# Attention scores from two halves of PE's rows instead of stacked operands, with transfers, a square and norm steps at other times

## The chip, the cores and the metric

One core of a Trainium2 chip runs the whole program. The metric is the device time of one execution in microseconds (us). The kernel before was run three times: 1136.16, 1132.1 and 1135.2 us, so its median is 1135.2 us. One more execution was profiled; it took 1132.5 us.

## The reference, cut to what matters

```python
q_rot, k_rot = (rotate(q), rotate(k))            # q, k, v: (4, 8, 576, 64) float32
scores = scale * np.matmul(q_rot, k_rot.transpose(0, 1, 3, 2))
scores = scores - np.max(scores, axis=-1, keepdims=True)
attn = np.exp(scores)
attn = attn / (np.sum(attn, axis=-1, keepdims=True) + 1e-09)
x = np.matmul(attn, v)                           # then to 2304 tokens x 512
xn = x / rms * rms_g
x = (silu(xn @ w_gate) * (xn @ w_val)) @ w_out   # d_ff 1536
x = (((x @ w1) * (x @ w2)) @ w3) @ w_out2        # d_ff 1024
```

q, k, v and the result are float32; most weights arrive as float64 and are converted on the chip. For the accuracy of float32 on PE, the kernel splits an operand into a rounded part ("hi") and the rest ("lo") and adds the products hi*hi, hi*lo and lo*hi (the tuple `PASS`).

## The kernel before, in words

**Stages.** The attention runs first, over 16 pairs of heads (two heads of 64 columns lie one under the other on the 128 partitions). Then the gated layer runs over 6 blocks of 384 tokens (lines 789 to 997; block 0 in two halves with block 1 between them), each with 12 columns n of 128 features: `pair_mm` is 24 matmuls, `second` 12. The products with w1, w2, w3 and w_out2 follow.

**One pair of heads.** POOL rotates q and k two pairs ahead (steps ra to rd). PE turns the result (q0p, q1p, q2p), ACT writes the hi part to `xs` and DVE the lo part to `ys` (the h and l steps), both in one tile `xy`. q occupies columns 0 to 703 of it, k the last 576. Then transfers of SP's queue build the operands of the scores. `q1d` (line 437) makes the stack of q, `qst`: for a head, hi on 64 rows and lo on the other 64. `q2d` (line 447) makes the stack of k, `ks`: hi on both halves of the rows, and lo on both halves. Each of the two steps issues four transfers. Pair 0 takes part of this by six copies of ACT and DVE instead (lines 728 to 734).

**Scores.** A pair has nine tiles of 128 queries: t = 0 to 3 of head 0, t = 5 to 8 of head 1, and t = 4 with what is left of both heads. The step S (line 471) makes a tile's 576 scores in two column halves `hf` of 288, each in its own PSUM bank. With the stacks, two matmuls over all 128 rows per half give the four products hi*hi, lo*hi, hi*lo and lo*lo: four matmuls a tile, eight for t = 4, 640 in all. M is the row maximum (DVE, line 487), E the exponential with its sum (ACT, line 493), T, H and Lo turn and split the tile (PE, ACT, DVE, lines 499 to 507), PV multiplies with v (line 555), X scales the result (POOL, line 612) and XD stores it.

**Order.** In the attention the order of every engine and of SP's queue is written out by hand. `ORDER` gives each step of a pair a time in units of one tile (nine to a pair); steps in q and v run one pair ahead, ra to rd, lq and lv two. `ONCE` does it for single steps: WF.u fetches the weight unit u, NX loads the rows of the first norm block, sq2 squares one of them. Of the steps that issue transfers, lq stands at 0.641, q1d at 5.817, q2d at 6.798, lv at 16.571 and XD at 17.967 (in the next pair's count 7.57 and 8.97); NX stands at 48.023 (pair 5, 3.02) and WF.5 at 94.711 (pair 10, 4.71), the other WF outside 0.5 to 7.2 of their pairs. The entry fixes only who stands before whom on an engine or in the queue. An instruction whose inputs are late holds up whatever stands behind it on the same engine or queue.

After the attention a scheduler orders the work by the order of the program, and gives a tile its buffer when one of its pool is free. The norm of block i+1 (`norm_steps`: load, three squares `sq`, `rst` and `nwt` for 1/rms, three scalings `zz`, line 668, and then xp, xh, xl three times) is cut by `NORM_AT` over the columns n of block i, for i = 2 to 4. The jobs of `JOBS` convert later weights (wo, w3, ws) and form sums of x (`sums`, lines 900 to 928) beside the blocks. The rows that a norm step loads, the outputs of a block and the tiles that the sums store to xsD share three buffers (pool `x2`, tag `o`). Each fetched weight goes through one of three raw buffers (`wst`) and each conversion through three `wt` buffers.

Of the kernel before, what the change touches and what calls it, by code (L numbers as in the profile page):

```python
# [9 lines left out]
F32R = mybir.dt.float32r  # L10
# [30 lines left out]
WARM = (22, 2, 3, 17)  # L41
NORM_AT = {5: (0, 1), 6: (1, 4), 7: (4, 6), 8: (6, 9), 9: (9, 12), 10: (12, 15), 11: (15, 18)}

# [17 lines left out]
def f(ap):  # L61
    return ap.bitcast(F32)
# [3 lines left out]
def kernel(  # L66
# [21 lines left out]
    nc = tc.nc  # L88
    B, H, S, D = q.shape
# [8 lines left out]
    HS = S // 2  # L98
# [57 lines left out]
    xy_p = pool("xy", 1)  # L156
    st_p = pool("st", 2)
# [117 lines left out]
    st = [0, 0]  # L275
# [20 lines left out]
    PASS = ((0, 0), (0, 1), (1, 0))  # L296
# [50 lines left out]
    part = {}  # L347
# [50 lines left out]
    QW = 704  # L398
    xy = xy_p.tile([128, 2, QW + S], F32R, name="xy")
    xs, ys = xy[:, 0], xy[:, 1]  # L400
    qst = [st_p.tile([128, 2, QW], F32R, name=f"qs{i}", bufs=1) for i in range(2)]
    qps = {}

    def two(a):
        return a[:, 576:832].rearrange("p (a b) -> p a b", a=2)[:, :, 0:64]

    def qt(g):

        n = [1, 4, 4][g]
# [8 lines left out]

        def qh(p):
            nc.scalar.copy(out=xs[:, c] if g else two(xs), in_=qps[p, g])  # L420

        def ql(p):
            hi, lo = (xs[:, c], ys[:, c]) if g else (two(xs), two(ys))
            nc.vector.tensor_tensor(out=lo, in0=qps.pop((p, g)), in1=f(hi), op=ALU.subtract)
# [6 lines left out]

    def move(mv):
        for o, i in mv:
            nc.sync.dma_start(out=f(o), in_=f(i))

    @step
    def q1d(p):
        qs = qst[p % 2]
        sl = slice(0, 640)
        sa = sl  # L440
        if p == 0:
            sa = slice(512, 640)
        move([(qs[0:64, 0, sa], xs[0:64, sa]), (qs[64:128, 0, sa], ys[0:64, sa]),
              (qs[64:128, 1, sl], xs[64:128, sl]), (qs[0:64, 1, sl], ys[64:128, sl])])

    @step
    def q2d(p):
        new_ks(p)
        ks = stacks[p]
        sl = slice(QW, QW + S)  # L450
        move([(ks[a:a + 64, 2 * h:2 * h + 2], xy[64 * h:64 * h + 64, :, sl]) for h in range(1 if p == 0 else 0, 2) for a in (0, 64)])

    def new_ks(p):
        if p not in stacks:
            stacks[p] = st_p.tile([128, 4, S], F32R, tag="ks", name="ks")

    s_ps, s_max, p_sb, sums, t_ps, l_ps, pv_ps, osb, xt, o_ps, rs_t = [{} for _ in range(11)]

    def hr(t):
        return (0, t) if t < 4 else (1, t - 5)  # L460
# [9 lines left out]
    def tile_steps(t):  # L470
        def S_(p):
            qs, ks = qst[p % 2], stacks[p]
            ps = ps_s.tile([128, 2, 512], F32, tag="s", name="s")
            if t == 4:
                mm = [(qs[:, h, 512 + 64 * h:640 + 64 * h], ks[:, 2 * h + i]) for h in range(2) for i in range(2)]
            else:
                h, r = hr(t)
                mm = [(qs[:, h, r * 128:(r + 1) * 128], ks[:, 2 * h + i]) for i in range(2)]
            n = len(mm)
            for hf in range(2):  # L480
                for i, (l, r_) in enumerate(mm):
                    nc.tensor.matmul(ps[:, hf, 0:HS], lhsT=l, rhs=r_[:, hf * HS:(hf + 1) * HS], start=(i == 0), stop=(i == n - 1))  # L482
            s_ps[p, t] = ps
# [216 lines left out]
    load_v(0)  # L700
    nc.vector.memset(f(xy[:, :, 512:576]), 0.0)
    for qs in qst:
        nc.vector.memset(f(qs[:, :, 640:QW]), 0.0)
    junk = const.tile([128, 1], F32, name="junk")
# [13 lines left out]
    for n_ in ("ra", "rb", "rc", "rd"):  # L718
        part[n_](1)
    new_ks(0)  # L720
    ks, sl = stacks[0], slice(QW, QW + S)
    for i, n_ in enumerate(("q2p", "q0p", "q1p")):
        part[n_](0)
        if i < 2:
            warm(i + 1)
    for n_ in ("q2h", "q0h", "q2l", "q0l", "q2d"):
        part[n_](0)
    nc.scalar.copy(out=ks[0:64, 0], in_=xs[0:64, sl])
    nc.vector.tensor_copy(out=ks[0:64, 1], in_=ys[0:64, sl])
    part["q1h"](0), part["q1l"](0)  # L730
    nc.scalar.copy(out=qst[0][0:64, 0, 0:512], in_=xs[0:64, 0:512])
    nc.vector.tensor_copy(out=ks[64:128, 1], in_=ys[0:64, sl])
    nc.scalar.copy(out=ks[64:128, 0], in_=xs[0:64, sl])
    nc.vector.tensor_copy(out=qst[0][64:128, 0, 0:512], in_=ys[0:64, 0:512])
    for n_ in ("q1d", "vh", "vl"):
        part[n_](0)
# [519 lines left out]
```

## Time and profile before

| | value |
|---|---|
| median of 3 runs | 1135.2 us (1132.1 to 1136.16) |
| profiled execution | 1132.5 us, span of its instructions 1130.7 us |
| mean granted clock of PE | 0.991 |
| PE matmul busy | 1085.4 us (96%), 6627 matmuls |
| DVE busy | 693.6 us (61%) |
| ACT busy | 558.3 us (49%) |
| POOL busy | 218.6 us (19%) |
| DMA | 183.52 MB, mean 162 GB/s |

An engine's share is a mean over stages with different limits: POOL works almost only in the attention, and DVE is near full there and half idle later. So the rows below are taken by stretch. Matmuls overlap one another, and the page says that a busy PE is not PE at its peak; the distance from one group of matmuls to the next in the chain of waits is the better measure of what one costs.

### The profile page before, as it was taken

The numbers are of one execution on the slowest core, as the hardware profiler recorded it, in microseconds if no ns is written. First come the engines' busy times: TensorE is split into PE (matmuls) and PEld (weight loads), VectorE is DVE, ScalarE is ACT, GpSimd is POOL, SyncE is SP. The second block draws the span as 40 slices with busy tenths as digits, with TensorE's granted clock in tenths as the row PEclk, the third lists the DMA queues.
The fourth block names the chain that finished last, engine by engine and source line by source line (L and its number), as shares of the span: only waits on it lengthen the run. The fifth ranks groups of instructions, "written<-read, shape, count | busy, mean of one in ns | idle before, by whom it ended". The sixth has DMA issues, their size and how long they took to land.

```text
span 1130.7 us, 18269 instructions
## 1 busy us (share of the span) xinstructions
PE 1085.4 (96%) x6627; PEld 1044.5 (92%) x6627; DVE 693.6 (61%) x1278; ACT 558.3 (49%) x1241; POOL 218.6 (19%) x191
## 2 busy tenths in 40 slices
PE   7899899799998999999899999999999999999998
PEld 6899899799997999999899999999999999987886
DVE  6999999799879883256666456653353442433221
ACT  4798898698875552234342243323454433323221
POOL 5777677579510000000000000000000000000000
PEclk9999999999999999999899999999999999999999
DMA  7677776767435640149476177554752324703451
GB/s 198 158 189 187 188 174 173 180 163 182 117 124 171 192 159 1 36 171 331 152 252 197 55 259 253 195 183 158 292 198 83 121 84 151 259 15 109 157 168 56
DMA packets 124698, 183.52 MB, mean 162 GB/s; under 512 B 18624, under 2 KB 85696, under 8 KB 124608
## 3 DMA queue, kind: packets, MB, share of 16 engines
q1 hardware_dynamic: 124608, 182.35, 53.2%
q8 instruction: 53, 0.87, 0.3%
q14 instruction: 37, 0.30, 0.1%
HBM read 101.63 MB, written 52.17 MB: 136 GB/s over the span
## 4 chain that ended last, share of the span: by engine, by line
PE 65%; DMA 14%; DVE 11%; issue 3%; ACT 2%; SPq 2%; POOL 2%; POOLq 0%; DVEq 0%; ACTq 0%
PE mm L305 16%; PE ps L1049 14%; PE ps L1190 9%; PE acc L813 8%; PE s L482 5%; PE ps L1152 4%; PE pv L555 3%; PE tp L499 3%; DMA wsD<-wt 3%; DMA wraw<-in_moe_w_val_dram 2%; DMA ks<-xy 2%; DVE nm L487 2%; DVE wt L233 1%; DMA woD<-wt 1%; DVE pt L507 1%
## 5 line engine op out<-in xcount | busy, mean ns | idle before, releaser
L305 PE MATMUL mm<-xc,wgv 128*128 128x384 f32 x1728 | 319.7, 337 | 3.2 <-ACT wgv L242 2.0
L305 PEld LDWEIGHTS mm<-xc,wgv 128*128 128x128 f32 x1728 | 302.3, 189 | 5.0 <-ACT wgv L242 3.2
L1049 PE MATMUL ps<-xs,cw 128*128 128x384 f32 x1008 | 175.9, 334 | 0.3 <-DMA xs<-xsD 0.3
L1049 PEld LDWEIGHTS ps<-xs,cw 128*128 128x128 f32 x1008 | 174.6, 188 | 1.0 <-DMA xs<-xsD 0.7
L813 PE MATMUL acc<-us,wo 128*128 128x384 f32 x864 | 166.8, 336 | 4.0 <-ACT us L104 3.6
L813 PEld LDWEIGHTS acc<-us,wo 128*128 128x128 f32 x864 | 150.4, 188 | 6.7 <-ACT us L104 5.6
L482 PE MATMUL s<-ks,qs 128*128 128x288 f32 x640 | 125.1, 324 | 17.0 <-DMA ks<-xy 7.6
L487 DVE TENSOR_REDUCE nm<-s 128x1 f32<-128x576 f32 x144 | 108.0, 750 | 17.8 <-PE s L482 16.1
L493 ACT ACTIVATE p<-s,nm 128x576 f32<-128x576 f32 x144 | 107.5, 746 | 21.2 <-DVE nm L487 20.5
L482 PEld LDWEIGHTS s<-ks,qs 128*128 128x128 f32 x640 | 94.3, 198 | 20.6 <-issue 12.5
L1190 PE MATMUL ps<-wp,us 128*128 128x512 f32 x432 | 98.2, 389 | 1.4 <-ACT us L104 1.4
L1190 PEld LDWEIGHTS ps<-wp,us 128*128 128x128 f32 x432 | 81.0, 188 | 18.6 <-ACT us L104 1.8
L507 DVE TENSOR_TENSOR pt<-tp,pt 128x512 fp32r<-128x512 f32 x144 | 94.7, 682 | 1.8 <-ACT pt L503 1.3
L104 ACT CAST us<-u 128x384 fp32r<-128x384 f32 x72 | 36.9, 512 | 112.5 <-DVE u L317 107.1
L317 DVE SCALAR_TENSOR_TENSOR u<-mm,sg 128x384 f32<-128x384 f32 x72 | 39.9, 555 | 82.5 <-PE mm L305 77.3
L555 PE MATMUL pv<-pt,vs 128*128 128x288 f32 x512 | 81.5, 301 | 2.4 <-DVE pt L507 2.4
L503 ACT CAST pt<-tp 128x512 fp32r<-128x512 f32 x144 | 82.5, 585 | 2.7 <-PE tp L499 1.7
L499 PE MATMUL tp<-idn,p 128*128 128x128 f32 x576 | 83.1, 277 | 0.6 <-DVE lt L537 0.5
L555 PEld LDWEIGHTS pv<-pt,vs 128*128 128x128 f32 x512 | 71.3, 189 | 2.9 <-DVE pt L507 2.9
L499 PEld LDWEIGHTS tp<-idn,p 128*128 128x128 f32 x576 | 68.9, 143 | 1.9 <-PE s L482 0.7
L315 ACT ACTIVATE sg<-mm 128x384 f32<-128x384 f32 x72 | 35.2, 489 | 65.5 <-PE mm L305 64.5
L1039 DVE TENSOR_TENSOR gv<-ps,gv 128x384 f32<-128x384 f32 x48 | 26.7, 556 | 54.9 <-PE ps L1049 34.2
(138 smaller groups left out, 1358.0 us busy)
## 6 DMA issues: line engine op xcount, KB each, us to landing
ks<-xy SPq DMA_DIRECT2D x62, 288.0 KB, 5.0
wraw<-in_moe_w_dram SPq DMA_DIRECT2D x32, 512.0 KB, 5.0
xsD<-xo SPq DMA_DIRECT2D x28, 384.0 KB, 3.8
xs<-xsD SPq DMA_DIRECT2D x14, 768.0 KB, 7.7
wraw<-in_moe_w_out_dram SPq DMA_DIRECT2D x20, 512.0 KB, 4.4
qs<-xy SPq DMA_DIRECT2D x62, 160.0 KB, 2.9
uD<-gv SPq DMA_DIRECT2D x12, 768.0 KB, 3.6
gv<-uD SPq DMA_DIRECT2D x24, 384.0 KB, 4.3
```

Of the source, the lines that this page charges most:

```text
L305: nc.tensor.matmul(ps[:, 0:CH], lhsT=w[:, a, s, c * 128:(c + 1) * 128], rhs=x[:, b_, c, :], start=(i == 0), stop=(i == 3 * KC - 1))
L482: nc.tensor.matmul(ps[:, hf, 0:HS], lhsT=l, rhs=r_[:, hf * HS:(hf + 1) * HS], start=(i == 0), stop=(i == n - 1))
L487: nc.vector.tensor_reduce(out=nm, in_=s_ps[p, t][:, :, 0:HS], axis=AX.XY, op=ALU.max, negate=True)
L493: nc.scalar.activation(out=pp.rearrange("p (a b) -> p a b", a=2), in_=s_ps.pop((p, t))[:, :, 0:HS], func=AF.Exp, bias=s_max.pop((p, t)), s ...
L499: nc.tensor.transpose(ps[:, c, :], p_sb[p, t][:, LF + c * 128:LF + (c + 1) * 128], idn)
L503: lastins["act"] = nc.scalar.copy(out=hi, in_=src)
L507: lastins["dve"] = nc.vector.tensor_tensor(out=lo, in0=src, in1=f(hi), op=ALU.subtract)
L555: nc.tensor.matmul(ps[:, 0:HS], lhsT=l.rearrange("p s d -> p (s d)"), rhs=r, start=(i == 0), stop=(i == 8))
L813: nc.tensor.matmul(acc[o][:, 0:CH], lhsT=wo[kind, n][:, a, o * 128:(o + 1) * 128], rhs=us[:, b_], start=(n == first and s == 0), stop=(n = ...
L1049: nc.tensor.matmul(b[ch], lhsT=w[i][:, p_, c * 128:(c + 1) * 128], rhs=x[i][:, r, c], start=(first and ch != 1 and n == 0), stop=(n == 5), ...
L1152: nc.tensor.matmul(p_, lhsT=t[a][:, c], rhs=woc[c][:, b_], start=(i == 0), stop=(i == 3 * NJ - 1))
L1190: nc.tensor.matmul(ac[o], lhsT=us[j // 2][:, a, j % 2, o * 128:(o + 1) * 128], rhs=wp[j][:, b_], start=(j == 0 and s == 0), stop=(j == NJ ...
```

## The change

The scores are computed from q and k where they were written. `xyt` holds two tiles in place of one `xy`, taken in turn by pairs. The stacks `qst` and `ks` are gone. `q1d` and `q2d` now issue two transfers each, which copy the tile with its two halves of rows exchanged into `stacks[p]`. A tile of scores takes the three products of `PASS`, each over 64 rows. For all pairs but the first, and for t = 4 of the first, column half 0 reads rows 0 to 63 and column half 1 rows 64 to 127: one of the two from the tile itself, the other from the exchanged copy. For t = 0 to 3 and 5 to 8 of pair 0 both column halves read the rows of their own head in the tile. That makes six matmuls a tile, twelve for t = 4, 960 in all, and lo*lo is no longer formed. The six copies of pair 0 are gone. `q1d` moves from 5.817 to 1.30 in `ORDER` and `q2d` from 6.798 to 1.45; `sq2` moves from 50.172 to 56.9 in `ONCE`. In `NORM_AT` the load of the rows moves from n = 5 to 3, the squares from 6 to 4, rst and nwt from 7 to 5, the scalings from 8 to 7.

```diff
@@ -22,7 +22,7 @@
     "E4": 2.051, "M5": 2.134, "Lo1": 2.149, "LH3": 2.471, "LL3": 2.5, "E5": 2.509, "H2": 2.685, "S6": 2.756,
     "M6": 2.821, "Lo2": 2.903, "T3": 3.161, "H3": 3.449, "S7": 3.7, "Lo3": 3.739, "E6": 4.29, "LP4": 4.29,
     "LH4": 4.474, "T4": 4.668, "S8": 4.729, "M7": 4.91, "H4": 5.08, "LL4": 5.462, "ra": 5.617, "E7": 5.756,
-    "q1d": 5.817, "M8": 6.032, "PV00": 6.229, "Lo4": 6.264, "rb": 6.41, "E8": 6.669, "q2d": 6.798, "OS00": 6.875,
+    "q1d": 1.30, "M8": 6.032, "PV00": 6.229, "Lo4": 6.264, "rb": 6.41, "E8": 6.669, "q2d": 1.45, "OS00": 6.875,
     "rc": 7.081, "LP8": 7.652, "rd": 7.781, "LH8": 8.249, "T5": 8.365, "T7": 8.385, "T8": 8.415, "H5": 8.594,
     "LL8": 8.681, "Lo5": 8.773, "T6": 8.824, "PV01": 8.959, "H7": 9.058, "H8": 9.103, "Lo7": 9.166, "H6": 9.477,
     "Lo8": 9.545, "OS01": 9.588, "vh": 9.685, "Lo6": 9.742, "PV11": 10.964, "vl": 11.081, "RS": 11.858, "OS11": 11.89,
@@ -32,14 +32,14 @@
 ONCE = {"WF.0": 0.058, "WF.1": 0.481, "W0.0": 2.871, "W1.0": 3.803, "W2.0": 4.815, "W0.1": 7.205, "W3.0": 7.711,
     "W1.1": 8.606, "WF.2": 16.22, "W2.1": 16.41, "W0.2": 19.818, "W3.1": 24.127, "WF.3": 26.556, "W4.0": 30.057,
     "W1.2": 32.027, "W5.0": 37.277, "W0.3": 37.9, "W2.2": 39.231, "W4.1": 41.145, "WF.4": 43.482, "NX": 48.023,
-    "W3.2": 49.378, "sq2": 50.172, "W0.4": 60.614, "W1.3": 61.7, "W5.1": 63.645, "W4.2": 66.556, "W2.3": 69.949,
+    "W3.2": 49.378, "sq2": 56.9, "W0.4": 60.614, "W1.3": 61.7, "W5.1": 63.645, "W4.2": 66.556, "W2.3": 69.949,
     "sq1": 70.293, "W5.2": 76.435, "sq0": 76.74, "W3.3": 77.538, "rst": 84.55, "W1.4": 88.619, "W2.4": 94.173,
     "WF.5": 94.711, "W4.3": 100.05, "W5.3": 101.185, "W3.4": 103.091, "W0.5": 104.358, "W1.5": 111.299, "nwt": 112.206,
     "W4.4": 114.592, "z0": 119.215, "W5.4": 121.51, "W2.5": 121.905, "z1": 125.342, "z2": 126.702, "W3.5": 132.583,
     "W4.5": 133.343, "xp1": 138.471, "xh1": 138.707, "xp0": 138.736, "W5.5": 138.782, "xh0": 139.246, "xl1": 139.435,
     "xl0": 139.778, "xp2": 140.495, "xh2": 141.275, "xl2": 141.913}
 WARM = (22, 2, 3, 17)
-NORM_AT = {5: (0, 1), 6: (1, 4), 7: (4, 6), 8: (6, 9), 9: (9, 12), 10: (12, 15), 11: (15, 18)}
+NORM_AT = {3: (0, 1), 4: (1, 4), 5: (4, 6), 7: (6, 9), 9: (9, 12), 10: (12, 15), 11: (15, 18)}
 
 SEGS = ((0, 0, 6), (1, 0, 12), (0, 6, 12))
 
@@ -396,9 +396,8 @@
         nc.gpsimd.tensor_tensor(out=vs[:, :, :, 1, :], in0=vraws.pop(p), in1=f(vs[:, :, :, 0, :]), op=ALU.subtract)
 
     QW = 704
-    xy = xy_p.tile([128, 2, QW + S], F32R, name="xy")
-    xs, ys = xy[:, 0], xy[:, 1]
-    qst = [st_p.tile([128, 2, QW], F32R, name=f"qs{i}", bufs=1) for i in range(2)]
+
+    xyt = [xy_p.tile([128, 2, QW + S], F32R, name=f"xy{i}") for i in range(2)]
     qps = {}
 
     def two(a):
@@ -417,9 +416,11 @@
             qps[p, g] = ps if g else ps[:, 0:128].rearrange("p (a b) -> p a b", a=2)
 
         def qh(p):
+            xs = xyt[p % 2][:, 0]
             nc.scalar.copy(out=xs[:, c] if g else two(xs), in_=qps[p, g])
 
         def ql(p):
+            xs, ys = xyt[p % 2][:, 0], xyt[p % 2][:, 1]
             hi, lo = (xs[:, c], ys[:, c]) if g else (two(xs), two(ys))
             nc.vector.tensor_tensor(out=lo, in0=qps.pop((p, g)), in1=f(hi), op=ALU.subtract)
 
@@ -429,30 +430,19 @@
     for g_ in range(3):
         qt(g_)
 
-    def move(mv):
-        for o, i in mv:
-            nc.sync.dma_start(out=f(o), in_=f(i))
+    def swap(p, sl):
+        if p not in stacks:
+            stacks[p] = st_p.tile([128, 2, QW + S], F32R, tag="st", name="st")
+        for h in range(2):
+            nc.sync.dma_start(out=f(stacks[p][64 - 64 * h:128 - 64 * h, :, sl]), in_=f(xyt[p % 2][64 * h:64 * h + 64, :, sl]))
 
     @step
     def q1d(p):
-        qs = qst[p % 2]
-        sl = slice(0, 640)
-        sa = sl
-        if p == 0:
-            sa = slice(512, 640)
-        move([(qs[0:64, 0, sa], xs[0:64, sa]), (qs[64:128, 0, sa], ys[0:64, sa]),
-              (qs[64:128, 1, sl], xs[64:128, sl]), (qs[0:64, 1, sl], ys[64:128, sl])])
+        swap(p, slice(0, QW))
 
     @step
     def q2d(p):
-        new_ks(p)
-        ks = stacks[p]
-        sl = slice(QW, QW + S)
-        move([(ks[a:a + 64, 2 * h:2 * h + 2], xy[64 * h:64 * h + 64, :, sl]) for h in range(1 if p == 0 else 0, 2) for a in (0, 64)])
-
-    def new_ks(p):
-        if p not in stacks:
-            stacks[p] = st_p.tile([128, 4, S], F32R, tag="ks", name="ks")
+        swap(p, slice(QW, QW + S))
 
     s_ps, s_max, p_sb, sums, t_ps, l_ps, pv_ps, osb, xt, o_ps, rs_t = [{} for _ in range(11)]
 
@@ -469,17 +459,17 @@
 
     def tile_steps(t):
         def S_(p):
-            qs, ks = qst[p % 2], stacks[p]
             ps = ps_s.tile([128, 2, 512], F32, tag="s", name="s")
-            if t == 4:
-                mm = [(qs[:, h, 512 + 64 * h:640 + 64 * h], ks[:, 2 * h + i]) for h in range(2) for i in range(2)]
-            else:
-                h, r = hr(t)
-                mm = [(qs[:, h, r * 128:(r + 1) * 128], ks[:, 2 * h + i]) for i in range(2)]
-            n = len(mm)
-            for hf in range(2):
-                for i, (l, r_) in enumerate(mm):
-                    nc.tensor.matmul(ps[:, hf, 0:HS], lhsT=l, rhs=r_[:, hf * HS:(hf + 1) * HS], start=(i == 0), stop=(i == n - 1))
+            hs = [(h, slice(512 + 64 * h, 640 + 64 * h)) for h in range(2)] if t == 4 else [(hr(t)[0], slice(hr(t)[1] * 128, (hr(t)[1] + 1) * 128))]
+            n = 3 * len(hs)
+
+            for i in range(n):
+                h, o = hs[i // 3]
+                a, b_ = PASS[i % 3]
+                for hf in range(2):
+                    g = hf if p or t > 3 else h
+                    src = (xyt[p % 2] if g == h else stacks[p])[64 * g:64 * g + 64]
+                    nc.tensor.matmul(ps[:, hf, 0:HS], lhsT=src[:, a, o], rhs=src[:, b_, QW + hf * HS:QW + (hf + 1) * HS], start=(i == 0), stop=(i == n - 1))
             s_ps[p, t] = ps
 
         def M_(p):
@@ -698,9 +688,9 @@
     load(0)
     load(1, xr_p.tile([128, NR, DM], F32, tag="xr", name="xr").rearrange("p r n -> p (r n)")[:, 0:18 * D].rearrange("p (h n d) -> p h n d", h=2, n=9))
     load_v(0)
-    nc.vector.memset(f(xy[:, :, 512:576]), 0.0)
-    for qs in qst:
-        nc.vector.memset(f(qs[:, :, 640:QW]), 0.0)
+    for xy in xyt:
+        for c in (512, 640):
+            nc.vector.memset(f(xy[:, :, c:c + 64]), 0.0)
     junk = const.tile([128, 1], F32, name="junk")
     nc.scalar.activation(out=junk, in_=one, func=AF.Exp)
 
@@ -717,22 +707,11 @@
             part[n_](0, eng, n)
     for n_ in ("ra", "rb", "rc", "rd"):
         part[n_](1)
-    new_ks(0)
-    ks, sl = stacks[0], slice(QW, QW + S)
     for i, n_ in enumerate(("q2p", "q0p", "q1p")):
         part[n_](0)
         if i < 2:
             warm(i + 1)
-    for n_ in ("q2h", "q0h", "q2l", "q0l", "q2d"):
-        part[n_](0)
-    nc.scalar.copy(out=ks[0:64, 0], in_=xs[0:64, sl])
-    nc.vector.tensor_copy(out=ks[0:64, 1], in_=ys[0:64, sl])
-    part["q1h"](0), part["q1l"](0)
-    nc.scalar.copy(out=qst[0][0:64, 0, 0:512], in_=xs[0:64, 0:512])
-    nc.vector.tensor_copy(out=ks[64:128, 1], in_=ys[0:64, sl])
-    nc.scalar.copy(out=ks[64:128, 0], in_=xs[0:64, sl])
-    nc.vector.tensor_copy(out=qst[0][64:128, 0, 0:512], in_=ys[0:64, 0:512])
-    for n_ in ("q1d", "vh", "vl"):
+    for n_ in ("q2h", "q0h", "q2l", "q0l", "q1h", "q1l", "q2d", "q1d", "vh", "vl"):
         part[n_](0)
     load_v(1, x_p.tile([128, 5, 2 * D], F32, tag="x", name="x").rearrange("p r n -> p (r n)").rearrange("p (h n d) -> p h n d", h=2, n=5))
     nc.sync.dma_start(out=g_sb, in_=rms_g.rearrange("(o n) -> o n", o=1).to_broadcast([128, DM]))
```

## Rows read from the trace of the kernel before

**Rows 1.** Windows by stage: stretch; busy us (instructions) per engine; clock; DMA share; GB/s.

```profile
16.02:22.68 6.66, 5.91 (x25) 5.54 (x25) 3.03 (x4) 2.97 (x7) 5.12 (x3) 1.00 0.85 196
22.68:306.49 283.81, 263.87 (x2071) 257.18 (x2069) 264.88 (x438) 243.08 (x600) 200.96 (x170) 0.98 0.71 176
...
329.42:1130.70 801.28, 784.34 (x4330) 752.24 (x4328) 395.29 (x779) 287.26 (x581) 0.00 (x0) 1.00 0.48 160
```

**Rows 2.** Windows of single pairs, from one t = 4 to the next; engines PE, PEld, DVE, ACT, POOL.

```profile
97.95:115.07 17.12, 17.12 (x143) 17.03 (x142) 16.67 (x31) 16.45 (x42) 12.39 (x11) 1.00 0.83 210
115.07:135.52 20.45, 17.49 (x144) 17.05 (x142) 17.79 (x31) 16.48 (x42) 13.99 (x11) 1.00 0.81 189
...
189.01:208.71 19.70, 17.52 (x143) 16.99 (x142) 19.39 (x33) 15.81 (x40) 12.54 (x10) 1.00 0.62 154
208.71:233.13 24.42, 19.83 (x143) 19.41 (x142) 17.08 (x31) 16.15 (x40) 12.69 (x9) 0.86 0.77 185
...
286.14:306.49 20.35, 17.99 (x140) 17.65 (x138) 18.17 (x32) 16.92 (x41) 10.52 (x14) 0.94 0.60 147
```

**Rows 3.** The chain of waits in an undisturbed pair: start us, us, what.

```profile
154.93 0.53 PE s L482 x4
155.46 0.44 PE lp L529 x4
155.89 1.20 PE pv L555 x9
157.09 0.44 PE tp L499 x4
```

**Rows 4.** Line 482, its instructions: duration ns min/median/max.

```profile
L482 PEld LDWEIGHTS s<-ks,qs x640: 186/188/338, 16.0 to 315.6; 128*128 128x128 f32 x160
L482 PE MATMUL s<-ks,qs x640: 289/295/609, 16.0 to 315.7; 128*128 128x288 f32 x160
```

**Rows 5.** Timeline of the start, DVE and PE: start us, us, instruction, idle before.

```profile
12.70 0.67 DVE L424 TENSOR_TENSOR xy<-qtp,xy 128x512 fp32r<-128x512 f32 x1
...
16.02 2.26 PE L482 MATMUL s<-ks,qs 128*128 128x288 f32 x8 [4.11 <-DVE qs L734]
```

**Rows 6.** Transfers of the operands: sizes and landing; SP's queue, PE, a window.

```profile
ks<-xy SPq DMA_DIRECT2D x62, 288.0 KB, 5.0
...
qs<-xy SPq DMA_DIRECT2D x62, 160.0 KB, 2.9
...
116.65 0.54 SPq L633 DMA_DIRECT2D xr<-xD  x1
...
119.81 4.08 SPq L434 DMA_DIRECT2D ks<-xy  x4
...
209.03 0.59 SPq L196 DMA_DIRECT2D wraw<-in_moe_w_out_dram  x1
...
128.65 0.77 PE L482 MATMUL s<-ks,qs 128*128 128x288 f32 x4 [2.96 <-DMA ks<-xy]
...
223.79 1.30 PE L482 MATMUL s<-ks,qs 128*128 128x288 f32 x4 [4.59 <-DMA ks<-xy]
...
206.56:223.70 17.14, 12.64 (x103) 12.37 (x101) 12.84 (x23) 12.25 (x31) 10.71 (x9) 0.96 1.00 236
```

**Rows 7.** The norm inside block 2: SP's queue, ACT, PE, then two pieces of the chain.

```profile
524.03 1.25 SPq L938 DMA_DIRECT2D xsD<-xo  x1
...
527.43 0.44 SPq L638 DMA_DIRECT2D xr<-xD  x1
...
533.51 0.63 ACT L663 ACTIVATE xc<-xr 128x512 fp32r<-128x512 f32 x1 [2.52 <-DMA xr<-xD]
...
547.65 1.12 PE L676 MATMUL xp<-idn,xr 128*128 128x128 f32 x4 [3.40 <-DVE xr L668]
...
548.76 6.37 PE mm L305 x24
...
555.57 4.17 PE mm L305 x24
```

## The prediction

> **What bounds the kernel now.** I read the windows by stage first, then single pairs, then the chain of waits inside a pair, and last the places where PE stood still.
>
> By stage [rows 1]: from 329 us on PE is busy 784 of 801 us, and DVE and ACT half of that or less. Nothing that the change does to the scores reaches this part; only the norm steps lie there. In the 15 pairs from 22.68 to 306.49 us PE (263.9), DVE (264.9) and ACT (243.1 of 283.8 us) are all near full. So the question there is not what PE gains, but who is next.
>
> By pair [rows 2]: the pair at 97.95 takes 17.12 us and PE is busy in all of it. DVE is busy 16.67 us of the same pair and ACT 16.45. The pair at 189.01 takes 19.70 us because DVE is busy 19.39; PE waits there. The pairs at 115.07, 208.71 and 286.14 have both engines idle: they wait for transfers. DVE's idle time over all 15 pairs is 283.8 - 264.9 = 18.9 us. That is the most that a faster PE and earlier transfers can give while DVE's own work stays as it is, and the change leaves that work alone after pair 0.
>
> What a tile of scores costs is read from the chain [rows 3]: four matmuls take 0.53 us from their start to the next group, 0.133 us each. The 295 ns of one matmul and the 188 ns of its load [rows 4] are latencies that overlap; they are not the pace.
>
> **The change, part by part.**
>
> *Scores.* A pair has ten tile-equivalents (t = 4 counts twice). Before, each costs 4 x 0.133 = 0.53 us. After, six matmuls; if the two halves of the rows work at the same time, they are three steps of 0.133 = 0.40 us, 1.33 us less per pair. No row shows two matmuls on different rows, nor any over 64 rows, so the cost has two ends. Low: 0.40. High: six in turn, 6 x 0.133 = 0.80 us. I take 0.40: the two halves share neither rows nor PSUM bank, and nothing in the instruction order makes one wait for the other. The Trainium skill (TensorEngine Tiling (Array Packing), Key Properties) says that tiles load and multiply in parallel; no run here shows it yet.
>
> How much of it is on the path: PE would need 17.1 - 1.3 = 15.8 us a pair, less than DVE's 16.6. So DVE ends a quiet pair, and a tile cheaper than about 0.48 us buys nothing more. The pair whose end DVE sets keeps 0.31 us of DVE idle time (19.70 - 19.39). With 0.35 us in every pair, 15 x 0.35 = 5.3 of the 18.9 us stay. The gain is 13.6 us, of which the transfers below are the larger part.
>
> *Transfers.* Per pair 4 x 160 + 4 x 288 = 1792 KB become two of 352 KB (64 rows, 2 x 704 words) and two of 288 KB: 1280 KB and four issues fewer. At the 236 GB/s of a full window [rows 6] the 512 KB are 2.2 us of a queue, and four issues cost SP some us as well (the four at 119.81 took 4.08). PE waited 2.96 us at 128.65 and 4.59 us at 223.79 for these transfers, and DVE's idle time in those two pairs is 2.66 and 7.34 us. In the queue the new times matter at two places only. lq (0.641) stays ahead, lv (7.57) and XD (8.97) stay behind in every pair. Of the single fetches NX (48.02, pair 5) and WF.5 (94.71, pair 10) fall between the old and the new places, and these are the very pairs that waited: the fetch of 768 KB at 116.65 and the weight unit at 209.03 stood ahead of the operands. Once the operands go first, the last of them lands earlier by 768 KB or 512 KB of fetch and by the 512 KB saved: 5.5 us in pair 5 and 4.4 us in pair 10 at 236 GB/s, against waits of PE of 2.96 and 4.59 us. Who is late next: NX's rows, but sq2 is moved almost seven tiles later too, and the weight unit, which is used pairs later. The dependence itself stays: every tile of pairs 1 to 15 needs the exchanged copy for one of its halves. No step of POOL moves. The pair at 286.14 (2.18 us of DVE idle) waits for a weight and I leave 1.8 us of it. So the pairs give 13.6 - 1.8 = 11.8, say **12 us**. Both ends: 0 (the waits come back elsewhere, scores cost the same) and 18.9.
>
> *Start.* Pair 0 loses six copies. S began at 16.02 after 4.11 us of idle PE, when DVE's last copy was done [rows 5]. Its last lo part (12.70, 0.67 us) is then the last input of S: 13.4 us, 2.6 earlier. Against it, four tiles of pair 0 now run six matmuls on the same rows, 2 x 0.133 us more each, or double that at the slow pace of these tiles (2.26 us for eight). In the first 6.66 us DVE and ACT are half idle [rows 1], so part is hidden. I take **2 us**; ends -1 and 2.6.
>
> *Norm.* In block 2, PE stood 3.40 us for the scalings at 547.65, after which 24 matmuls took 6.37 us where the next 24 took 4.17 [rows 7]: 3.40 + 2.20 = 5.6 us, and 0.7 for xp itself (1.12 us for what costs 0.44 elsewhere [rows 3]): 6.3 us. The rows were loaded at 527.43, right after the last store to xsD, and ACT waited 2.52 us for them at 533.51. A column n lasts 4.17 us for `pair_mm` and half of that for `second`, 6.26 us. The load and squares two columns earlier (12.5 us) and the scalings one earlier end a wait of 3.40 us. I take **6 us**; ends 0 (the three buffers come free no sooner) and 6.3. sq2, the memsets (one more, 0.16 us) and DVE's order cost nothing that is not covered: the later blocks leave DVE half idle.
>
> Sum: 12 + 2 + 6 = 20 us off the profiled 1132.5, so 1112.5. The median before, 1135.2, lies 2.7 us above that execution, and I carry this over: 1115 for the median after.
>
> **A rule that speaks against it.** In the chain, four turnings into 64 columns (lp) sit between scores and pv and cost 0.44 us, as much as four over 128 columns [rows 3]; a change of shape in columns costs nothing that shows. The Trainium skill (TensorEngine Tiling (Array Packing), Key Properties) says that a change of the tiling mode drains the engine. The row disagrees for columns; for rows it is open, and it is a rival below.
>
> **Rivals.**
>
> *The halves work in turn, and it ends slower.* Each tile costs 0.80 us, PE needs 17.1 + 2.7 = 19.8 us a pair, and 15 pairs take 15 x 19.9 = 298.5 us, 14.7 more than now. Start and norm take 2 + 6 off: 1132.5 + 14.7 - 8 = 1139.2, a median of **1142**. It decides from the tile at which PE needs (283.8 + 8)/15 = 19.4 us a pair: 0.53 + (19.4 - 17.1)/10 = 0.76 us. For it: no row shows concurrency. Against: different rows, different banks.
>
> *The loads go in turn.* Every step of tp loads 128 columns and takes 0.11 us (0.44 for four), so six loads need at most 0.66 us a tile. PE then needs 18.4 us a pair; pairs that DVE holds longer keep their time; the 15 take about 282. Sum: 1132.5 - 1.8 - 8 = 1122.7, median **1125**. The Trainium skill (TensorE: Matmul & The Clock Gate, LDWEIGHTS) makes a load's time depend on its columns alone, 107 ns for 128; by it the tile would be 0.64 us, close to the same.
>
> *A drain at each change between 128 and 64 rows.* A matmul's latency beyond its pace is 0.295 - 0.133 = 0.16 us. Two per tile make 9 x 0.32 = 2.9 us a pair: 15.8 + 2.9 = 18.7, the pairs about 285 us, some 1 more than now: 1132.5 + 1 - 8 = 1125.5, median **1128**, and more where a drain costs more than that.
>
> *The norm's rows hold the three buffers.* Loaded before the sums have stored, they keep all three until xp at n = 9. The 14 stores of the sums (the last at 524.03) then wait, and with them raw and wt buffers and the wo jobs: some 35 us of conversion shift into later blocks. PE gets its 6 us in block 2, but pays where a late job stands ahead of a gate on ACT or DVE. Price: from half to all of the 20 us gained, **1125 to 1135**. For it: the load came right after the last store, so it did wait for buffers. Against: the jobs have room, DVE being half idle after 329 us [rows 1].
>
> *Nothing changes in the pairs*, because another input (weights, rotation on POOL) is late at the same places: 1132.5 - 8 = 1124.5, median **1127**.
>
> **How the numbers follow.** Forecast 0.55 (its own range 1107 to 1121). Halves in turn 0.13. Loads in turn 0.12. Drain 0.08. Buffers 0.08. Nothing in the pairs 0.04. Half a per cent, 5.7 us, is about what a measurement of this kernel can tell from no change: faster is below 1129.5, slower above 1140.9. Forecast, loads, the unchanged pairs and part of drain and buffers are faster: 0.73. Halves in turn and the worst drain are slower: 0.15. The rest, 0.12, is the same. The low end takes all upper gains, 18.9 + 2.6 + 6.3 = 27.8 us, a median of 1107, less the 3 us by which the runs before lay below their median: 1104. The high end takes in all rivals up to just short of the halves in turn: 1139.
>
> **What would show it.** Right: four groups of scores in the chain at 0.40 us; quiet pairs near 16.9 us with DVE as their end; no wait of S for an operand at the pairs 6 and 11; S at about 13.4 us; xp in block 2 without a wait for the scalings. Wrong: scores at 0.64 us or more per tile, PE busy in whole pairs of 18 us and longer; gaps of some 0.16 us around each tile; the wait of S under another name; stores to xsD after 540 us and gates waiting behind jobs; or pairs that stay at 18.9 us on average with DVE no fuller than now.

## The result: 1.4% slower, and the profile after

The changed kernel takes 1150.1 us (median of 4 runs, 1144.4 to 1151.0) against 1133.7 us for the kernel before (1128.3 to 1136.2): a ratio of 1.014, 95% interval 1.0105 to 1.0176. The forecast was 1115 us and the range ended at 1139. The profiled execution took 1149.5 us with a span of 1147.7, 17.0 us more than the span before.

One sentence on the change above is wrong: in pair 0 only t = 0 to 3 read the rows of their own head for both column halves; t = 4 to 8 take the two halves of the rows, as all later pairs do.

Where the span went is read from the first matmul of each stage (us, one profiled execution each; the runs behind the two kernels are told below):

| kernel | first S | blocks | w1, w2 | last stage | span |
|---|---|---|---|---|---|
| before | 16.0 | 326.0 | 799.6 | 1027.9 | 1130.7 |
| after | 11.6 | 331.3 | 810.9 | 1044.9 | 1147.7 |
| a_scores | 12.6 | 331.8 | 805.8 | 1038.9 | 1141.7 |
| a_oldnorm | 12.2 | 332.8 | 805.5 | 1040.9 | 1143.7 |
| a_late | 13.0 | 335.0 | 805.3 | 1036.0 | 1138.9 |
| b_newnorm | 16.1 | 330.1 | 806.3 | 1040.9 | 1143.7 |
| b_nn_late | 16.1 | 326.1 | 799.5 | 1030.4 | 1133.3 |
| b_times | 16.5 | 314.2 | 783.4 | 1014.9 | 1117.8 |

The 17.0 us are 5.3 up to the start of the blocks, 6.0 in the blocks (479.6 for 473.6) and 5.7 in the stage with w1 and w2 (234.0 for 228.3). That last stage takes from 228.3 to 235.4 us in these eight executions. In after and in b_newnorm PE waits there for rows `xs` that are loaded from xsD, 4.5 us and 5.8 us in all; in before it waits 0.3 for them, in a_late 1.2. So the edits to the norm have a part in it. What else varies there is not laid to any edit.

First the pairs: windows of after, the first over the same stretch as in [rows 1], then single pairs from one t = 4 to the next as in [rows 2], the last from the blocks on.

```profile
22.68:306.49 283.81, 277.25 (x2317) 231.36 (x2316) 257.68 (x428) 238.59 (x584) 193.02 (x164) 0.99 0.59 147
...
61.50:80.44 18.94, 18.94 (x162) 15.90 (x162) 16.80 (x29) 16.32 (x41) 12.63 (x10) 1.00 0.65 164
...
195.50:215.71 20.21, 19.02 (x161) 15.90 (x161) 19.08 (x32) 15.97 (x40) 12.61 (x10) 1.00 0.51 122
...
329.42:1147.70 818.28, 792.17 (x4366) 756.03 (x4364) 399.90 (x788) 293.19 (x591) 1.60 (x1) 1.00 0.48 158
```

A quiet pair, one in which PE never stands still, takes 18.94 us instead of 17.12 [rows 2]: PE is busy in all of it while DVE, at 16.80, has time to spare. PE sets the pace, not DVE. The DMA share of the stretch fell from 0.71 to 0.59 [rows 1].

Next the tiles of scores, the timeline of PE. Before, three groups of an undisturbed pair:

```profile
157.28 0.79 PE L482 MATMUL s<-ks,qs 128*128 128x288 f32 x4
157.91 0.60 PE L499 MATMUL tp<-idn,p 128*128 128x128 f32 x4
158.26 0.77 PE L482 MATMUL s<-ks,qs 128*128 128x288 f32 x4
```

After, the same kind of place (each line one matmul on 64 rows; `st` is the exchanged copy):

```profile
143.08 0.60 PE L489 MATMUL tp<-idn,p 128*128 128x128 f32 x4
143.61 0.40 PE L472 MATMUL s<-st 64*128 64x288 f32 x1
143.62 0.40 PE L472 MATMUL s<-xy 64*128 64x288 f32 x1
143.85 0.29 PE L472 MATMUL s<-st 64*128 64x288 f32 x1
...
143.98 0.28 PE L472 MATMUL s<-st 64*128 64x288 f32 x1
...
144.22 0.66 PE L489 MATMUL tp<-idn,p 128*128 128x128 f32 x4
144.80 0.40 PE L472 MATMUL s<-st 64*128 64x288 f32 x1
```

The two halves of the rows do work side by side: their matmuls start 10 ns apart, and the third pair follows the second after 0.13 us, as forecast. But around them time is lost three times: 0.53 us from tp to S where it was 0.35, 0.24 us from the first step to the second, and 0.23 us from the last step to tp. From one S to the next it is 1.19 us where it was 0.98.

### The profile page after: what moved, and what is told of

The parts are those of the page before. It is cut to its first block, busy times and chain, and to the rows that moved or that the text cites. A ratio compares the mean times of both kernels' runs of the same rounds, so it can differ in the third digit from the quotient of the medians.

```text
span 1147.7 us, 18756 instructions
## 1 busy us (share of the span) xinstructions
PE 1110.1 (97%) x6947; PEld 1022.9 (89%) x6947; DVE 690.0 (60%) x1276; ACT 560.0 (49%) x1238; POOL 215.7 (19%) x191
## 5 line engine op out<-in xcount | busy, mean ns | idle before, releaser
L472 PE MATMUL s<-xy 64*128 64x288 f32 x492 | 107.0, 332 | 2.0 <-ACT p L483 1.3
L472 PE MATMUL s<-st 64*128 64x288 f32 x468 | 99.8, 326 | 2.7 <-DMA st<-xy 1.9
L472 PEld LDWEIGHTS s<-xy 64*128 64x128 f32 x492 | 73.2, 194 | 16.4 <-issue 6.6
L489 PE MATMUL tp<-idn,p 128*128 128x128 f32 x576 | 85.4, 281 | 0.1
L545 PE MATMUL pv<-pt,vs 128*128 128x288 f32 x512 | 83.9, 306 | 0.1
L472 PEld LDWEIGHTS s<-st 64*128 64x128 f32 x468 | 67.0, 187 | 13.9 <-issue 5.6
L489 PEld LDWEIGHTS tp<-idn,p 128*128 128x128 f32 x576 | 65.9, 143 | 8.7 <-issue 7.6
```

The lines of the kernel that those rows point to most:

```text
L472: nc.tensor.matmul(ps[:, hf, 0:HS], lhsT=src[:, a, o], rhs=src[:, b_, QW + hf * HS:QW + (hf + 1) * HS], start=(i == 0), stop=(i == n - 1))
L489: nc.tensor.transpose(ps[:, c, :], p_sb[p, t][:, LF + c * 128:LF + (c + 1) * 128], idn)
L545: nc.tensor.matmul(ps[:, 0:HS], lhsT=l.rearrange("p s d -> p (s d)"), rhs=r, start=(i == 0), stop=(i == 8))
```

## The experiments

Each kernel was timed beside the kernel before, whose median was 1130.4 to 1132.9 us in these runs; 'before with' names an edit of the kernel before, 'after with' one of the changed kernel.

### The parts taken apart

**b_times**: before with the new times of q1d, q2d and sq2 alone.

```diff
-    "q1d": 5.817, ... "q2d": 6.798, ... "sq2": 50.172,
+    "q1d": 1.30, ... "q2d": 1.45, ... "sq2": 56.9,
```

> The kernel before with the new times of q1d, q2d and sq2 alone. If the fetches ahead of the operands made the waits of pairs 6 and 11, these waits go (2.96 and 4.59 us of PE and the slow stretch behind the second) and the time is 1124 to 1128 us. Rival: another input is late at the same places, 1134 us.

Measured 1120.5 us, ratio 0.992 (0.989 to 0.995); once more as **b_times_again**, 1122.9 us, 0.992 (0.990 to 0.994).

> The kernel before with the new times of q1d, q2d and sq2 alone, once more, beside the others: 1118 to 1123, a ratio of 0.990 to 0.994.

The two pairs that waited for their transfers [rows 2, 6] end after 17.63 and 17.42 us (windows of b_times):

```profile
113.37:131.00 17.63, 17.56 (x143) 17.06 (x141) 17.34 (x30) 15.84 (x40) 12.14 (x10) 1.00 0.83 218
205.66:223.08 17.42, 17.42 (x142) 17.05 (x141) 17.12 (x30) 15.83 (x40) 10.35 (x9) 1.00 0.86 223
```

The second gains 7.0 us (24.42 before), more than the wait of 4.59 us that is gone: the granted clock of PE, 0.86 in that pair before, is 1.00 here. So the new times are worth 8 to 10 us as long as the scores are the old ones, of 6 to 10 expected, and this kernel is faster than both. The share of sq2's move was not measured by itself.

**a_oldnorm**: after with the old NORM_AT. **b_newnorm**: before with the new one.

```diff
-NORM_AT = {5: (0, 1), 6: (1, 4), 7: (4, 6), 8: (6, 9), 9: (9, 12), ...
+NORM_AT = {3: (0, 1), 4: (1, 4), 5: (4, 6), 7: (6, 9), 9: (9, 12), ...
```

> The changed kernel with the old NORM_AT. If the norm's early load holds the three buffers (theory B), the 14 stores of the sums come before the load again, the waits of PE at 600 to 640 us and from 770 to 840 us go, and the 5.6 us wait for the scalings in block 2 comes back: about 12 us less than the changed kernel, 1138 us. Rival: the waits come from the attention that ends 5 us later, and the time stays at 1150 us.

> The kernel before with the new NORM_AT alone. Theory B: no wait for the scalings at 547 us, but stores of the sums after 540 us and gates waiting behind late jobs: 1134 + 12 = 1146 us. Rival (the early norm is good by itself, as predicted): 1128 us.

Measured 1143.5 us (1.0105, 1.006 to 1.015) and 1144.3 us (1.0104, 1.006 to 1.015). The new NORM_AT costs time in the kernel before: 13.9 us, near what was expected. In the changed kernel it is 1150.1 - 1143.5 = 6.6 us by medians, of 12 expected. These two were timed beside different runs of before, and their ratios, 1.014 and 1.0105, have intervals that overlap, so this figure is rough.

**a_scores**: after with the old times and the old NORM_AT, so the new scores, the exchanged copy and the new start alone.

```diff
-    "q1d": 1.30, ... "q2d": 1.45, ... "sq2": 56.9,
+    "q1d": 5.817, ... "q2d": 6.798, ... "sq2": 50.172,
-NORM_AT = {3: (0, 1), 4: (1, 4), 5: (4, 6), 7: (6, 9), ...
+NORM_AT = {5: (0, 1), 6: (1, 4), 7: (4, 6), 8: (6, 9), ...
```

> The changed kernel with the old times of q1d, q2d and sq2 and the old NORM_AT: the new scores, the swapped copy and the new start alone. By the theory that every change of rows costs PE about 0.3 us a tile, PE is the end of every pair (18.9 us) and no DVE idle time is left to take it up: over 1130.4 us at least 10 us more, and what waits for transfers remain at pairs 5 and 10 come on top, 1143 to 1155. Rival (the loss of the scores lies in their early transfers, not in PE): 1128 to 1136.

Measured 1143.0 us, ratio 1.0105 (1.008 to 1.013). This is the time of a_oldnorm: with the new scores the new times give nothing. The pair that waited longest before already ends after a quiet pair's 18.94 us with q1d and q2d at their old places (window of a_scores):

```profile
216.85:235.79 18.94, 18.94 (x162) 15.90 (x161) 17.29 (x30) 15.97 (x40) 12.48 (x7) 1.00 0.77 198
```

### What a change of rows costs

**b_mix64**: before, with the second product of each column half over 64 rows (t = 4 apart), and the two matmuls over 128 rows first. The same four matmuls a tile, no two on different halves, and one trip from 128 rows to 64 and back.

```diff
+                o = slice(64 * h, 64 * h + 64)
-                mm = [(qs[:, h, ...], ks[:, 2 * h + i]) for i in range(2)]
+                mm = [(qs[:, h, ...], ks[:, 2 * h]), (qs[o, h, ...], ks[o, 2 * h + 1])]
-            for hf in range(2):
-                for i, (l, r_) in enumerate(mm):
+            for i, (l, r_) in enumerate(mm):
+                for hf in range(2):
```

> The kernel before; for every tile but t = 4 the second product of each column half runs over 64 rows (hi of q with lo of k) in place of 128, after both of the first. Count and columns of the matmuls stay, lo*lo is left out of these tiles. If a change between 128 and 64 rows drains PE (theory D: about 0.3 us a tile more, read from the changed kernel), 8 tiles a pair make some 2.4 us, PE is the bound in every pair and the time is 1155 to 1170 us. If the loss in the changed kernel came from six loads or from two matmuls at once, nothing changes here: 1134 us.

Measured 1157.5 us, ratio 1.023 (1.019 to 1.027). Its quiet pair takes 19.89 us, with PE busy in all of it. The order within a tile changes here too; the next run keeps that of before.

**b_mix64x2**: the same without the last four lines of that diff, so that the rows go 128, 64, 128, 64: two trips a tile.

> The kernel before with the second product of each column half over 64 rows (t = 4 apart; lo*lo is left out there), in the order of the kernel before: 128, 64, 128, 64 rows in a tile, two round trips where the run that took 1157.5 us had one (128, 128, 64, 64). If each round trip costs what that run showed in a quiet pair, 19.88 - 17.12 = 2.76 us over 8 tiles = 0.345 us: a quiet pair of 22.6 us and 1157.5 + 15 x 2.76 = 1199, 1185 to 1205. If the cost is one per matmul over 64 rows or one per tile, whatever the order: 1155 to 1162.

Measured 1200.9 us (one run). Windows of a quiet pair and the timeline of PE, b_mix64 first:

```profile
168.85:188.74 19.89, 19.89 (x143) 17.26 (x142) 16.86 (x30) 17.29 (x43) 13.72 (x15) 1.00 0.63 154
...
145.04 0.96 PE L483 MATMUL s<-ks,qs 128*128 128x288 f32 x4
145.93 0.66 PE L500 MATMUL tp<-idn,p 128*128 128x128 f32 x4
146.34 0.97 PE L483 MATMUL s<-ks,qs 128*128 128x288 f32 x4
```

b_mix64x2:

```profile
120.62:143.60 22.98, 22.98 (x143) 18.40 (x142) 17.36 (x29) 17.07 (x42) 12.60 (x10) 1.00 0.61 153
...
149.31 1.35 PE L483 MATMUL s<-ks,qs 128*128 128x288 f32 x4
150.60 0.65 PE L500 MATMUL tp<-idn,p 128*128 128x128 f32 x4
151.01 1.35 PE L483 MATMUL s<-ks,qs 128*128 128x288 f32 x4
```

From one S to the next: 0.98 us with no trip, 1.30 with one, 1.70 with two. By pairs: (19.89 - 17.12) / 8 = 0.35 us for the first trip of a tile, (22.98 - 19.89) / 8 = 0.39 for the second. The cost is paid per change of rows, and it needs neither more matmuls nor two halves at work. The changed kernel pays one trip in each of nine tiles: 15.79 us (17.12 less 1.33 for the cheaper steps) + 9 x 0.35 = 18.94 us, which is its quiet pair.

**a_hfmajor**: after, with the three products of column half 0 issued before the three of half 1.

```diff
-            for i in range(n):
+            for hf in range(2):
...
-                for hf in range(2):
+                for i in range(n):
```

> The changed kernel with the six matmuls of a tile in another order: the three of column half 0, on rows 0 to 63, and then the three of half 1, on rows 64 to 127; the same matmuls and the same changes of rows per tile. If the two halves of the rows work side by side only because neighbours in the order use different halves: six steps in turn, 0.4 us more per tile equivalent, 4 us a pair, 15 pairs 60 us: 1190 to 1215. If PE lets later matmuls pass earlier ones, or if the loads of the weights set the pace: 1145 to 1160.

Measured 1152.1 us (one run). A quiet pair takes 19.34 us, 0.04 more per tile. Its window and the timeline of PE:

```profile
60.22:79.56 19.34, 19.34 (x162) 16.31 (x161) 16.76 (x30) 16.42 (x41) 12.61 (x10) 1.00 0.64 161
...
144.38 0.40 PE L472 MATMUL s<-st 64*128 64x288 f32 x1
144.39 0.40 PE L472 MATMUL s<-xy 64*128 64x288 f32 x1
```

In this tile the copy `st` holds the rows of half 0, so the fourth matmul in the program's order starts with the first. The side-by-side work doesn't hang on the order that the program gives within a tile. Whether PE itself lets them pass, or gets them in another order than the program's, the trace doesn't tell.

### The norm and its buffers

The queue of SP in block 2 of after (`xr` are the norm's rows, `xsD` the stores of the sums), where [rows 7] had all stores done at 525 us and the rows behind them:

```profile
508.90 2.05 SPq L917 DMA_DIRECT2D xsD<-xo  x2
511.36 0.33 SPq L628 DMA_DIRECT2D xr<-xD  x1
511.74 0.44 SPq L917 DMA_DIRECT2D xsD<-xo  x1
513.16 2.45 SPq L628 DMA_DIRECT2D xr<-xD  x2
547.80 0.37 SPq L917 DMA_DIRECT2D xsD<-xo  x1
```

The three rows take the three buffers, and the fourth of the 14 stores comes some 35 us later, when xp has freed one. In block 2 itself PE gains what was forecast (timeline of PE, against [rows 7]): xp without a wait, and 4.41 us for the 24 matmuls behind it.

```profile
546.03 0.60 PE L666 MATMUL xp<-idn,xr 128*128 128x128 f32 x4
546.39 4.41 PE L305 MATMUL mm<-xc,wgv 128*128 128x384 f32 x24
```

What had made the 24 matmuls slow before is the granted clock: PE had stood still for 3.40 us, and behind that its clock was at the lower of its two levels, 1.2 of 2.4 GHz (a window of before, then one of after):

```profile
548.00:553.00 5.00, 5.00 (x18) 5.00 (x17) 1.61 (x3) 0.95 (x2) 0.00 (x0) 0.50 0.12 48
...
546.00:555.00 9.00, 9.00 (x57) 8.93 (x55) 4.79 (x9) 4.04 (x8) 0.00 (x0) 1.00 0.40 133
```

PE pays for it in block 3, where the conversions of weights now come late. ACT waits for a raw weight, and the gate `us` that PE needs stands behind it (ACT, then PE, of after):

```profile
600.87 0.70 ACT L820 ACTIVATE wraw<-wraw 128x512 f32<-128x512 f32 x1 [3.16 <-DMA wraw<-in_moe_w_dram]
601.47 0.49 ACT L104 CAST us<-u 128x384 fp32r<-128x384 f32 x1
...
602.02 0.62 PE L792 MATMUL acc<-us,wo 128*128 128x384 f32 x2 [0.40 <-ACT us L104]
603.84 2.03 PE L792 MATMUL acc<-us,wo 128*128 128x384 f32 x10 [0.85 <-DVE us L105]
```

The sums of block 4 wait for the norm's rows in the same way, and more is paid behind them: PE waits for `us` between 772 and 807 us, and then for the rows that the next stage loads from xsD (waits of PE from 795 to 1045 us, before and after):

```profile
PE ps L1049 <- DMA xs<-xsD: 0.3, 1, 0.3
PE ps L1028 <- DMA xs<-xsD: 4.5, 4, 2.3
```

**b_nn_late**: b_newnorm with the sums of x behind the norm's last xp. **a_late**: the same edit in the changed kernel.

```diff
-        + [(i, 2 + c, ("sums", i // 2 - 1, c)) for i in (2, 4) for c in range(2)]
+        + [(i, 11 + c, ("sums", i // 2 - 1, c)) for i in (2, 4) for c in range(2)]
```

> The kernel before with the new NORM_AT, and with the two jobs that form the sums of x in blocks 2 and 4 moved from columns 2 and 3 to columns 11 and 12, behind the last xp of the block. With the new NORM_AT alone the kernel took 1144.3 against 1130.4 us. Theory (the early rows hold the three buffers and the stores of the sums wait for them): now nothing waits for the buffers, the stores of the sums come in one stretch after the block's xp, the waits of second at 601 to 640 us go, and of the 13.9 us at least half goes: 1128 to 1137. Rival (the norm steps themselves, earlier, stand ahead of the gates on ACT and DVE): the sums make no difference, 1142 to 1146, and the waits for us stay.

> The changed kernel (1150.1) with the sums of x at columns 11 and 12 of blocks 2 and 4, behind the norm's xp. If the 6.6 us that the new NORM_AT costs here are the stores of the sums waiting for the three buffers: 1141 to 1146, as with the old NORM_AT (1143.5) or a little under. If they are something else: 1148 to 1152.

Measured 1132.5 us for b_nn_late, ratio 1.000 (0.997 to 1.003): all of the 13.9 us is gone. And 1134.9 us for a_late, ratio 1.002 (1.0005 to 1.004): 15.1 us less than the changed kernel by medians, more than expected. (Its profiled execution was the slowest of its ten, at 1140.6 us.) What PE waited for from 480 to 830 us (summed us, times, longest), after first:

```profile
PE acc L792 <- ACT us L104: 6.3, 6, 1.8
PE ps L1028 <- DMA xs<-xsD: 4.0, 3, 2.3
PE acc L792 <- DVE us L105: 2.8, 5, 0.9
```

a_late:

```profile
PE acc L792 <- ACT us L104: 2.3, 1, 2.3
PE acc L792 <- DVE us L105: 1.3, 2, 0.7
PE ps L1028 <- DMA xs<-xsD: 0.5, 1, 0.5
```

So the loss was the stores of the sums waiting for the buffers that the norm's rows hold, not the norm steps themselves.

### The start, and versions that might be the best

**b_t_start**: b_times with the first two tiles of pair 0 taken straight from q and k, as the change does.

```diff
+            if p == 0 and t < 2:
+                mm = [((xs, ys)[a][0:64, ...], (xs, ys)[b_][0:64, QW:QW + S]) for a, b_ in PASS]
```

> The kernel before with the new times, and with the first two tiles of pair 0 taken as three products of the 64 rows of head 0 straight from q and k, as the change does it; the stack is used from the third tile on, so the six copies stay but S no longer waits for them. If the start was bound by these copies: the first S at 11.6 instead of 16.0 us and 2 to 4 us off 1120.5, so 1116.5 to 1118.5. If DVE is the bound of the first pair (the copies still stand ahead of the first maximum): S at 11.6 and the time unchanged, 1119.5 to 1121.5.

Measured 1125.3 us, ratio 0.996 (0.994 to 0.998): no gain over b_times, and above both times that were expected. Its S starts at 12.76 us instead of 16.55, and at the next pair nothing is left of that (PE of b_t_start, then of b_times, then of after):

```profile
35.20 1.30 PE L484 MATMUL s<-ks,qs 128*128 128x288 f32 x4 [4.72 <-ACT osb L562]
```

```profile
35.30 1.33 PE L482 MATMUL s<-ks,qs 128*128 128x288 f32 x4 [2.21 <-ACT p L493]
```

```profile
11.57 3.25 PE L472 MATMUL s<-xy 64*128 64x288 f32 x12 [0.68 <-ACT xy L420]
...
33.87 0.37 PE L472 MATMUL s<-st 64*128 64x288 f32 x1 [1.91 <-DMA st<-xy]
```

Three more kernels put b_times together with the norm: **b_t_nn_late** (new NORM_AT, late sums), **b_t_late** (old NORM_AT, late sums) and **b_t_mid** (late sums, and this):

```diff
+NORM_AT = {4: (0, 1), 5: (1, 4), 6: (4, 6), 8: (6, 9), 9: (9, 12), ...
```

> The kernel before with the new times of q1d, q2d and sq2 (alone 1120.5 us), with the new NORM_AT and with the sums at columns 11 and 12. Theory of the buffers: the norm steps now give the 3 to 6 us that the prediction wanted of block 2, or at least cost nothing: 1114 to 1122. Rival: 1130 to 1135, as the new NORM_AT costs 10 to 14 us wherever the sums stand.

> The kernel before with the new times of q1d, q2d and sq2, the old NORM_AT, and the sums of x at columns 11 and 12 of blocks 2 and 4. The load of the norm's rows (column 5) then has no store of a sum ahead of it; if it was the buffers that made it wait, block 2 loses its stops of 2.1 to 2.4 us and the time is 1114 to 1119 against 1120.5 with the sums at 2 and 3. If the sums at the later place stand ahead of the gates of the next block, 1120 to 1126.

> As b_t_late, with the norm's load, squares, rst and scalings one column earlier than of old (4, 5, 6, 8; the new NORM_AT has 3, 4, 5, 7). Without the sums in the way an earlier norm should cost nothing: 1114 to 1120. If the norm steps on ACT and DVE hold up the gates wherever they stand before xp: 1121 to 1126.

Measured 1123.4 us (0.9925, 0.990 to 0.995), 1124.8 us (0.994, 0.992 to 0.996) and 1121.8 us (0.991, 0.9885 to 0.994). None can be told from b_times, and none gives the gain that was hoped for: with the sums out of the way the norm's place is worth nothing there, and late sums alone gain nothing. No version is faster beyond the noise than before with the new times: 0.992 of before, some 2% under the changed kernel.

## Why the prediction was wrong, point by point

**Scores: the step that failed first.** The prediction took 0.40 us a tile, from three steps of 0.133. The steps are right and the side-by-side work too; the Trainium skill's sentence that tiles work in parallel (TensorEngine Tiling (Array Packing), Key Properties) agrees with the starts 10 ns apart. What failed is that the 0.40 put the change between 128 and 64 rows at nothing. No row of the kernel before shows a matmul over 64 rows; the nearest, the change in columns that costs nothing that shows [rows 3], was held against a cost, and a cost in rows was left to a rival. That change costs 0.35 us a tile. The Trainium skill's rule in the same section, that a change of the tiling mode drains the engine, agrees with such a cost; that PE drains is not itself seen, and b_mix64 and b_mix64x2 show the price, for which the page has no figure. The rival had the mechanism right: two latencies of 0.16 us, a pair of 18.7 us against 18.94 measured; it stood at a chance of 0.08, and its time of 1128 was missed with the others, since the norm cost time too.

**Who is next.** "DVE ends a quiet pair" fell with it: PE is busy in all of a quiet pair, and DVE is not.

**Transfers.** Right for the kernel before: the waits at pairs 5 and 10 go and 8 to 10 us come off. Wrong as a term of this sum: in pairs of 18.94 us the smaller transfers come in time at the old places too. What the waits cost before is taken up by PE's slower pace and by the smaller transfers together. From pair 1 to pair 14, 13 pairs, can be read from the matmuls that turn q ahead of t = 4 (two of before, two of after):

```profile
43.15 0.60 PE L416 MATMUL qtp<-idn,rot 128*128 128x128 f32 x4
285.78 0.60 PE L416 MATMUL qtp<-idn,rot 128*128 128x128 f32 x4
42.04 0.60 PE L415 MATMUL qtp<-idn,rot 128*128 128x128 f32 x4
292.08 0.60 PE L415 MATMUL qtp<-idn,rot 128*128 128x128 f32 x4
```

That is 242.6 and 250.0 us. Before, it is 13 x 17.12 = 222.6 and 20.1 of waits, those of PE for DVE among them; after, 13 x 18.94 = 246.2 and 3.8 of waits. The slower pace of 23.7 us and the 16.3 us of waits saved leave +7.4 us where the prediction had -12 for its 15 pairs. How much the pace does by itself is seen in b_mix64, slower still and with the old transfers at the old places: pair 5 is almost quiet there (20.17 us), but pair 10 still takes 24.01 us and waits (a window, then PE):

```profile
229.48:253.49 24.01, 21.65 (x143) 18.59 (x142) 18.59 (x29) 16.12 (x40) 12.12 (x7) 0.93 0.76 175
...
243.74 0.95 PE L483 MATMUL s<-ks,qs 128*128 128x288 f32 x4 [2.36 <-DMA ks<-xy]
```

**Start.** S starts at 11.6 us, earlier than the 13.4 forecast: its first product needs only the hi parts, and the line of after in the section on the start shows it behind ACT, which writes them. But the 2 us were not kept: of 4.4 us earlier, 1.1 are left at pair 1, where a tile waits 1.91 us for the exchanged copy, and b_t_start shows no gain in the kernel before. The start of S is not what holds up the second pair.

**Norm.** The local part was right: the wait of 3.40 us and the slow 24 matmuls went. The rival of the three buffers was right about the rest, down to the 35 us: PE paid from block 3 on for the conversions and the loads behind the late stores, 6.6 us in all here (a rough figure, as said) and 13.9 in the kernel before. With the sums moved behind the norm, a_late is 8.5 us under a_oldnorm. That this lies near the 6 us forecast is no confirmation: in the table the blocks give 2.4 of it (470.3 for 472.7) and the stage with w1 and w2 gives 4.7, while the attention takes 2.2 more. In the kernel before the same pair of edits gives nothing (b_nn_late), and why the two differ was not settled.

**The sum.** By medians: scores and start +12.4 us (a_scores against its runs of before), new times +0.4 in the changed kernel, norm +6.6; together 19.4, where the comparison of the two kernels has 16.4 (the runs of before timed beside it were up to 3 us slower than those beside the others). Of the scores' 12.4, the attention shows about 6 in the table; most of the rest lies in the stage with w1 and w2 (233.1 for 228.3), where PE waits 4.0 us for results of DVE that it doesn't wait for before; why DVE is late there stays open. By the table, the part up to the blocks took 5.3 us more where the forecast had 14 less, and all behind it 11.7 more where the forecast had 6 less. The rivals were priced one at a time, each with the gains of the other parts left in; the drain and the buffers came together.

## What to carry to other kernels

Where matmuls on part of the rows stand among matmuls on all of them, as here, count the changes of rows per tile and charge each round trip (here 0.35 us) before counting what the side-by-side work saves. A load that is moved ahead takes its buffer ahead as well: look at who else takes buffers from that pool in between, and move that behind it first. A wait that is removed is worth nothing where another edit has already covered it, by a slower pace or by smaller transfers, so terms of a sum must be worked out against the kernel that the other edits leave.

## What the runs showed of the hardware that was not expected

A trip from 128 rows to 64 and back costs PE 0.35 us for the first of a tile and 0.39 for a second, also where products over 128 and over 64 rows are added up in one bank; a change from 128 to 64 columns shows no such cost [rows 3]. Matmuls on different halves of the rows need not alternate in the program: in a_hfmajor the fourth in the program's order started 10 ns after the first, and the order within the tile was worth only 0.04 us. A wait of PE can cost more than its length: behind 3.40 us of standing still the granted clock was 0.50 for 5 us, and 24 matmuls took 6.37 us where the next 24 took 4.17 [rows 7].
